# Two product steps moved behind each value product, and three transfers of the last head group issued at other places, in a gated attention and feed-forward kernel

## The chip, the cores and the metric

One Trainium2 chip, one of its cores. The number is the device time of one execution in microseconds. TensorE (PE) does the matrix products, VectorE (DVE), ScalarE (ACT) and GpSimd (POOL) the elementwise work, and SyncE (SP) only issues transfers. Each engine works through its own instructions strictly in the order in which the program issues them; an instruction that waits holds up everything behind it on that engine. POOL issues transfers too, so a transfer that must wait for its source stands in front of POOL's next elementwise work.

## What is computed

```python
def _A_ref(x, wqkv, wo):                     # S=2048, D=512
    H = 32; Dh = D // H; W = 256             # causal, window of 256
    scores = jnp.einsum("bhqd,bhkd->bhqk", q, k) * (Dh ** -0.5)
    mask = (idx[:, None] - idx[None, :] >= 0) & (idx[:, None] - idx[None, :] < W)
    p = _softmax(jnp.where(mask[None, None], scores, -1e9), axis=-1)
    return (heads of p @ v side by side) @ wo
def _B_ref(x, w_gate, w_up, w_down):         # F=1792
    return (_silu(x @ w_gate) * (x @ w_up)) @ w_down
g = _sigmoid((x * gate_w).sum(-1, keepdims=True))
return g * a + (1 - g) * b
```

All of it is in float32; the kernel splits operands into a high and a low half (`split`, line 67) and makes three products for one.

## The kernel before

Three stages follow each other. The **first** (to about 165 us) makes values, queries and keys. The **second** (to about 640 us) runs the attention of the 32 heads in 8 groups `g` of 4, and, between the attention's instructions, the products of x with `w_gate` and `w_up` for the feed-forward part. The **third** multiplies the hidden tiles with `w_down`, the attention with `wo`, and mixes both.

**The order of the second stage is written out by hand** (lines 793 to 826). `t` counts blocks of 128 positions over all groups, 16 a group; the last group, `g` = 7, is `t` = 112 to 127, and `t` = 128 only ends it. A block has four **ticks** (`hd` = 0 to 3); tick `k` is 4`t` + `hd`. In a tick the program issues, in this order: one score tile for finding the row maxima of the next group (`s1`, `stage1`, line 595, product into a bank `pc`, reduced by DVE in line 597); one score tile of this group (`s2`, `stage2`, line 634, into one of two banks `pd`, then ACT's exponential in line 636 into a tile `pt`, then POOL's masks on a pair of heads in lines 638 and 641); some **steps** of the feed-forward products (line 556); and at the end whatever was booked for this tick (`tick_end`). In the last group there is no `s1`, and `s2` comes two at a time in ticks 0 and 2.

**A step** is two products of 512 columns, one on each half of PE's 128 rows ("lanes"). The score tiles also take half of the rows each, `s1` and `s2` opposite halves. `DEAL` (lines 791, 792) says how many steps each tick gets; in the first block of four they are `1, 2, 0, 1` for groups 0 to 6, and two in every tick for the last group.

**The value product** (`av`, line 656) multiplies the masked `pt` tiles of up to six blocks with the values, for 512 positions at a time. It is issued in tick 1 of every fourth block, behind that tick's steps. It fills two banks: one of the `pc` kind and, before the last group, one of the two `pd` banks that `s2` uses. `evacuate` (line 661) follows: ACT copies the second bank to `ob` (line 667), the two are added to `oe` (for `g` = 7 by DVE, line 669), and POOL issues the store of `oe` to the tensor `od` (line 675). So 32 value products are made, 27 of them with a `pd` bank.

**Sums and inverses.** One row in 17 of what a value product makes is the softmax's sum. `invert` (line 454) reads the sums of 512 positions back from `od` (`den`, line 456), takes the reciprocal (line 458) and stores it to `rd` (line 459); both transfers are issued by POOL. In the last group `INV[c]` does this for chunks `c` = 0 and 1, booked at ticks 4(117 + 4`c`) + 3 and 12 ticks later (lines 766 to 768). The chunks 2 and 3 follow in the third stage.

**The odd sum.** `lanes` deals the feed-forward sums over two lanes of 64 rows. One sum is left over: its lane-1 half is made at the very start of the stage and put in the tensor `spill` (line 526); its lane-0 half comes at the very end (block 125 on). When its first product is issued, the program takes a `kept` buffer and has POOL load `spill` into it (lines 552, 553); `odd_end` adds the two (DVE, line 530).

**Also in POOL's queue in the last group:** the low halves of the last weights (`wl`, line 72), stores of the last unit's sums (line 501), and loads of `w_down` into buffers of the last weights (`wd_raw`, line 782), three of them booked for tick 502, in block 125. Two of those three go into the buffers (`wh`, `wl`) of the unit whose last step is the last step of the stage.

Of the kernel before, what the change touches and what calls it, by code (L numbers as in the profile page):

```python
# [9 lines left out]
F32 = mybir.dt.float32  # L10
# [6 lines left out]
P = 128  # L17
S, D, H, DH, W, F = 2048, 512, 32, 16, 256, 1792
NK = D // P
NB = S // P  # L20
CH = 512
NCH = S // CH
G = H // 4
# [10 lines left out]
def gated_mix(ctx, tc, xT, xn, wqk, wv, wo, wgu, wd, gw, out):  # L34
# [4 lines left out]
    nc = tc.nc  # L39
# [8 lines left out]
    od = dram.tile([G, P, S], F32, name="od")  # L48
    raws = dram.tile([NF, 2, NCH, P, CH], F32, name="raws")
    spill = dram.tile([P, CH], F32, name="spill")  # L50
# [36 lines left out]
    def run(gen, n=None):  # L87

        while n is None or n > 0:
            if next(gen, run) is run:  # L90
                break
            n = n and n - 1
# [19 lines left out]
    def bank(n):  # L112
        names = BANKS[n if isinstance(n, str) else ("pa", "pb", "pc", "pd")[n]]
        names.append(names.pop(0))
        return psum.tile([P, CH], F32, name=names[-1])
# [338 lines left out]
    def invert(c, pool):  # L454
        den = pool.tile([P, P], F32, name="den")
        nc.gpsimd.dma_start(den, shares[:, c * CH:(c + 1) * CH].rearrange("h (q i) -> h q i", q=4))
        yield
        nc.vector.reciprocal(den, den)
        nc.gpsimd.dma_start(rd[c].rearrange("h (q i) -> (h q) i", q=4), den)
        yield  # L460

# [6 lines left out]
    with ExitStack() as A:  # L468
        sm = A.enter_context(tc.tile_pool(name="sm", bufs=2))
        osb = A.enter_context(tc.tile_pool(name="osb", bufs=1))  # L470
        ptp = A.enter_context(tc.tile_pool(name="ptp", bufs=13, side="right"))

        def kept():
            return sm.tile([P, CH], F32, name="ev", bufs=EV)
# [5 lines left out]
        def later(n, *fs):  # L480
            AT.setdefault(NOW[0] + n, []).extend(fs)

        def at(k, *fs):
            AT.setdefault(k, []).extend(fs)
# [8 lines left out]
        def products(key, c):  # L493
            wh, wl = WT[key]
            return [(wt[:, k], xt[c][:, k]) for k in range(NK) for wt, xt in ((wh, xhi), (wh, xlo), (wl, xhi))]

        def copy_out(key, c, ps):
            place = kept()
            queue = nc.gpsimd if key == UNITS[-1] else nc.sync
            later(0, lambda: nc.scalar.copy(place, ps))  # L500
            later(3, lambda: queue.dma_start(raws[key[1], key[2], c], place))
# [10 lines left out]
        LAG, PART = 3 * NK + 6, []  # L512

        def lanes():


            turn, sums = 3 * NK, [(key, c) for key in UNITS[1:] for c in range(NCH)]
            odd = sums.pop(NCH - 1)
            ps, turned = {odd: bank("pa")}, {}
            rows = (sums + [odd], [odd] + [None] + sums)  # L520
            starts = [[turn * o for o in range(len(sums) + 1)], [0, turn] + [turn * o + LAG for o in range(len(sums))]]

            def odd_start(ps):
                place = kept()
                later(0, lambda: nc.scalar.copy(place, ps))
                later(3, lambda: nc.sync.dma_start(spill, place))

            def odd_end(ps):
                place, rest = kept(), PART.pop()
                later(0, lambda: nc.vector.tensor_tensor(out=place, in0=ps, in1=rest, op=ALU.add))  # L530
                later(3, lambda: nc.gpsimd.dma_start(raws[odd[0][1], odd[0][2], odd[1]], place))

            def items(lane):
                for at_, o in zip(starts[lane], rows[lane]):
                    while o and len(lines[lane]) < at_:
                        lines[lane].append(None)
                    if o:
                        lines[lane].extend((o, i) for i in range(turn))

            lines = [], []  # L540
            items(0)
            items(1)
            for both in zip_longest(*lines):
                for lane, item in enumerate(both):
                    if item is None:
                        continue
                    o, i = item
                    first = o is odd or not lane
                    if first and i == 0 and not (lane and o is odd):
                        ps[o] = bank("pa")  # L550
                        if o is odd:
                            PART.append(kept())
                            nc.gpsimd.dma_start(PART[0], spill)
                    w, x = products(*o)[i]
                    r = slice(64 * lane, 64 * lane + 64)
                    mm = nc.tensor.matmul(ps[o], w[r], x[r], start=first and i == 0,  # L556
                                          stop=(o is odd or bool(lane)) and i == turn - 1)
                    if not first and i == 0:
                        tc.add_manual_dep(mm.ins, BEHIND[turned.pop(o)].ins.name, SYNC, reason="the other rows are summed")
                    if i < turn - 1:  # L560
                        continue
                    if o is odd:
                        (odd_start if lane else odd_end)(ps.pop(o))
                    elif not lane:
                        turned[o] = len(BEHIND)
                    else:
                        copy_out(*o, ps.pop(o))
                        n = sums.index(o) + 1
                        if n == len(sums) or sums[n][0] != o[0]:
                            later(3, prepare)  # L570
                yield
# [89 lines left out]
        def evacuate(g, c):  # L661

            first, second = AV[g, c]
            lo = 0 if c else 64
            e = osb.tile([P, CH], F32, name="oe", bufs=2)
            o = osb.tile([P, CH], F32, name="ob")
            nc.scalar.copy(o[:, lo:], second[:, lo:])  # L667
            if g == G - 1:
                nc.vector.tensor_tensor(out=e[:, lo:], in0=first[:, lo:], in1=o[:, lo:], op=ALU.add)
                if lo:  # L670
                    nc.vector.tensor_copy(e[:, :lo], first[:, :lo])
            else:
                nc.vector.tensor_copy(e, first)
                nc.gpsimd.tensor_tensor(out=e[:, lo:], in0=e[:, lo:], in1=o[:, lo:], op=ALU.add)  # L674
            nc.gpsimd.dma_start(od[g, :, c * CH:(c + 1) * CH], e)

# [43 lines left out]
        def wd_early(k, f, piece):  # L722
            at(k, lambda: later(4, load_wd(f, pieces[piece], kept())))
# [33 lines left out]
        g7 = (G - 1) * NB  # L757
# [4 lines left out]
        for b in range(NB):  # L762
            at(4 * (17 + 4 * b) + 2, lambda b=b: gate_block(b))
        at(4 * (g7 + 2), gate_end)
        INV = [invert(c, osb) for c in range(2)]
        for c in range(2):
            for n in range(2):
                at(4 * (g7 + 5 + 4 * c) + 3 + 12 * n, lambda c=c: run(INV[c], 1))
        at(4 * g7, put_pieces)
        for m in range(8):  # L770
            wd_early(4 * (g7 + 1 + m) + 2, m, m)
        for n in range(2):
# [16 lines left out]
            spread(4 * (16 * g + 17) + 1, 1, stack(g + 2, 1))  # L789

        DEAL = [[[(hd + 1) * n // 4 - hd * n // 4 for hd in range(4)] for n in deal] for deal in ((4, 9, 9, 8), (8, 8, 8, 8))]
        DEAL[0][0] = 1, 2, 0, 1
        for t in range(G * NB + 1):
            g, i = divmod(t, NB)
            d, part = divmod(t, NSLOT)
            s1 = stage1(g + 1, i) if t < g7 else iter(())
            s2 = stage2(g, i) if t < G * NB else iter(())
            values = part == 0 and t > 0
            for hd in range(4):
                k = NOW[0] = NSLOT * t + hd  # L800
                if not (values and hd == 2):
                    run(s1, 1)
                if t < g7:
                    run(s2, 1)
                elif hd % 2 == 0:
                    run(s2, 2)
                if t == G * NB and hd == 0:
                    last_tile = tile_silu(2)
                    run(last_tile, 1)
                if t < G * NB:  # L810
                    run(steps, DEAL[t >= g7][part][hd])
                if hd == 1 and values:
                    run(s1, 1)
                    av(*divmod(d - 1, NCH))
                    while UNDER:
                        UNDER.pop(0)()
                    evacuate(*divmod(d - 1, NCH))
                tick_end()
            if i in (7, 15) and g + 1 < G:
                UNDER.append(lambda g=g, i=i: put_max(g + 1, i // 8))  # L820
            if t >= 10 and t % 4 == 2 and t + 6 < G * NB:
                load_v((t + 6) // 4)
# [196 lines left out]
```

## Time and profile before

| | us |
|---|---|
| median of 3 runs | 842.83 (842.41 to 843.29) |
| the profiled execution, as a run | 846.21 |
| its span, first to last instruction | 844.5 |
| PE busy | 824.5 |
| PEld (weight loads) busy | 692.8 |
| DVE, ACT, POOL busy | 552.2, 472.8, 402.5 |
| mean granted TensorE clock | 0.997 |

The profiled execution took 846.21 us, 1.71 more than its span and 3.38 more than the median run. Line numbers are those of the kernel before. In a row of the timeline stand start, duration, engine, line, operation, out<-in, shape, count and, in brackets, how long the engine was idle before it and what ended that. In a row of the waits stand who waited for whom, the total, how often, and the longest. A busy time of PE overlaps the next product's start, so PE's lost time is read from starts, not from the busy share.

### The profile page before, as it was taken

Reading aid. Unit: us, or ns where it says so; the run is one execution under the profiler, and the core shown is the slowest. Engines: PE = TensorE matmul, PEld = TensorE weight load, DVE = VectorE, ACT = ScalarE, POOL = GpSimd, SP = SyncE. Lnnn points to the kernel's source line nnn. Section 1 sums busy time; section 2 is a strip of 40 time slices with the busy share of each in tenths; the row PEclk is TensorE's granted clock in tenths of the full one; section 3 lists DMA queues with packets and bytes.
Section 4 is the critical chain, followed back from the end, with each engine's and each line's share of the span. In section 5 each row is a group of like instructions: output and inputs, shape, how many; then the busy total and the mean of one; then the engine's idle time right before and its main releaser. Section 6 shows DMA issues by size and latency. Waiting matters only on the chain.

```text
span 844.5 us, 20512 instructions
## 1 busy us (share of the span) xinstructions
PE 824.5 (98%) x7681; PEld 692.8 (82%) x7681; DVE 552.2 (65%) x1425; ACT 472.8 (56%) x956; POOL 402.5 (48%) x716
## 2 busy tenths in 40 slices
PE   9999999999999999999999999999987999999998
PEld 7888888888888888888888888888765888888886
DVE  5675554158786877878878778784473657564652
ACT  7454553222676776766767667676664563433431
POOL 5124441441465666766667666666664015352220
PEclk9999999999999999999999999999999999999999
DMA  8456676386534564545645455433638797878611
GB/s 295 142 174 224 231 263 217 132 274 198 169 117 153 194 205 149 191 147 199 205 158 185 154 165 180 148 122 114 209 117 297 279 283 218 258 228 256 204 59 50
DMA packets 80147, 159.70 MB, mean 189 GB/s; under 512 B 14960, under 2 KB 19440, under 8 KB 80048
## 3 DMA queue, kind: packets, MB, share of 16 engines
q1 hardware_dynamic: 68400, 127.18, 45.1%
q0 software_dynamic: 11072, 30.17, 11.0%
q8 instruction: 60, 0.98, 0.5%
q10 hardware_dynamic: 576, 1.05, 0.4%
q14 instruction: 39, 0.32, 0.1%
HBM read 93.32 MB, written 65.01 MB: 187 GB/s over the span
## 4 chain that ended last, share of the span: by engine, by line
PE 91%; POOL 2%; ACT 2%; issue 2%; DMA 1%; SPq 0%; DVE 0%; ACTq 0%; DVEq 0%; POOLq 0%
PE pa L556 20%; PE pb L556 10%; PE pd L634 6%; PE pc L656 4%; PE pd L381 4%; PE pb L381 4%; PE pa L381 4%; PE pd L83 3%; PE pc L595 3%; PE pc L83 3%; PE pc L82 3%; PE pc L81 3%; PE pd L82 3%; PE pd L81 3%; PE pb L656 2%
## 5 line engine op out<-in xcount | busy, mean ns | idle before, releaser
L636 ACT ACTIVATE pt<-pd 128x384 f32<-128x384 f32 (+2 forms) x512 | 233.0, 475 | 50.0 <-PE pc L595 12.5
L597 DVE CUSTOM_DVE_ANT_0 pc<-pc,mask 128x384 f32<-128x384 f32 (+2 forms) x322 | 172.4, 544 | 41.7 <-PE pc L595 22.2
L634 PE MATMUL pd<-q,k 64*128 64x384 f32 (+2 forms) x512 | 174.1, 352 | 9.5 <-ACT ob L667 6.8
L556 PE MATMUL pa<-xhi,wh 64*128 64x512 f32 x492 | 160.7, 398 | 0.0
L556 PE MATMUL pa<-xhi,wl 64*128 64x512 f32 x492 | 157.7, 393 | 0.0
L556 PE MATMUL pa<-xlo,wh 64*128 64x512 f32 x492 | 157.4, 393 | 0.0
L638 POOL TENSOR_SCALAR_AFFINE_SELECT pt<-pt 128x256 f32<-128x256 f32 x256 | 108.0, 422 | 75.9 <-ACT pt L636 74.1
L634 PEld LDWEIGHTS pd<-q,k 64*128 64x128 f32 x512 | 93.2, 184 | 35.2 <-ACT ob L667 14.8
L595 PE MATMUL pc<-k,q 63*128 63x384 f32 (+2 forms) x322 | 103.2, 327 | 0.0
L641 POOL TENSOR_SCALAR_AFFINE_SELECT pt<-pt 128x256 f32<-128x256 f32 x224 | 97.3, 434 | 0.0
L556 PE MATMUL pb<-xhi,wh 64*128 64x512 f32 x244 | 97.1, 398 | 0.0
L597 DVE CUSTOM_DVE_ANT_0 pb<-pb,mask 128x384 f32<-128x384 f32 (+2 forms) x158 | 86.2, 546 | 15.3 <-PE pb L595 10.0
L556 PE MATMUL pb<-xlo,wh 64*128 64x512 f32 x244 | 96.0, 394 | 0.0
L556 PE MATMUL pb<-xhi,wl 64*128 64x512 f32 x244 | 95.8, 392 | 0.0
L556 PEld LDWEIGHTS pa<-xhi,wh 64*128 64x128 f32 x492 | 80.2, 185 | 2.1 <-DVE mx L597 0.5
L556 PEld LDWEIGHTS pa<-xhi,wl 64*128 64x128 f32 x492 | 79.6, 185 | 1.7
L556 PEld LDWEIGHTS pa<-xlo,wh 64*128 64x128 f32 x492 | 79.5, 186 | 1.2
L904 DVE TENSOR_TENSOR sg<-got,sg 128x512 f32<-128x512 f32 x53 | 45.4, 857 | 46.2 <-ACT sg L903 38.7
L597 DVE DVE_READ_ACCUMULATOR2_ANT mx<- 128x1 f32 x512 | 72.5, 142 | 0.0
L656 PE MATMUL pd<-pt,vg 64*32 64x320 f32 (+4 forms) x1184 | 63.1, 346 | 0.0
L674 POOL TENSOR_TENSOR oe<-oe,ob 128x512 f32<-128x512 f32 (+1 forms) x28 | 35.1, 1254 | 55.9 <-ACT ob L667 52.4
L595 PEld LDWEIGHTS pc<-k,q 63*128 63x128 f32 x322 | 58.7, 184 | 3.6 <-DVE mx L597 0.4
(306 smaller groups left out, 2046.3 us busy)
## 6 DMA issues: line engine op xcount, KB each, us to landing
got<-raws SPq DMA_DIRECT2D x106, 256.0 KB
raws<-ev SPq DMA_DIRECT2D x91, 256.0 KB
q<-xd SPq DMA_DIRECT2D x96, 128.0 KB
k<-xd SPq DMA_DIRECT2D x96, 128.0 KB
xd<-cx SPq DMA_DIRECT2D x16, 512.0 KB
xd<-cy SPq DMA_DIRECT2D x16, 512.0 KB
od<-oe POOLq DMA_DIRECT2D x32, 256.0 KB, 3.1
raw<-wgu SPq DMA_DIRECT2D x25, 256.0 KB
```

The source lines that it names most:

```text
L81: nc.tensor.matmul(ps, lh, rh, start=start and i == 0, stop=False, skip_group_check=skip)
L82: nc.tensor.matmul(ps, lh, rl, start=False, stop=False, skip_group_check=skip)
L83: nc.tensor.matmul(ps, ll, rh, start=False, stop=stop and i == n - 1, skip_group_check=skip)
L381: nc.tensor.matmul(ps, l[:, w], r[:, k], start=n in (1, 2, 5) and k == m == 0, stop=k == 1 and m == 2, skip_group_check=True)
L556: mm = nc.tensor.matmul(ps[o], w[r], x[r], start=first and i == 0, stop=(o is odd or bool(lane)) and i == turn - 1)
L595: nc.tensor.matmul(ps[:, :n], QT[g % 2][pr][r, q0:q0 + P], KT[g % 2][pr][r, k0:k0 + n], start=True, stop=True)
L597: mx = nc.vector.tensor_tensor_reduce(out=ps[:, :n], in0=ps[:, :n], in1=mask[:, 3 * P - n:], scale=1.0, scalar=NEG, op0=ALU.add, op1=ALU.m ...
L634: nc.tensor.matmul(ps[:, :n], KT[g % 2][pr][r, k0:k0 + P], QT[g % 2][pr][r, k0:k0 + n], start=True, stop=True)
L636: BEHIND.append(nc.scalar.activation(pt[:, j, :n], ps[:, :n], AF.Exp, scale=SCALE))
L638: nc.gpsimd.affine_select(out=pt[:, :, :P], in_=pt[:, :, :P], pattern=[[0, 2], [1, P]], compare_op=ALU.is_ge, fill=0.0, base=0, channel_mu ...
L641: nc.gpsimd.affine_select(out=pt[:, :, 2 * P:], in_=pt[:, :, 2 * P:], pattern=[[0, 2], [-1, P]], compare_op=ALU.is_ge, fill=0.0, base=-1, ...
L656: nc.tensor.matmul(AV[g, c][h][32 * j:32 * j + 32, q0 - c * CH:q1 - c * CH], VG[4 * g + kb // 4][o, kb % 4, 17 * j:17 * j + 32], PT[g, kb, ...
```

## The change

Three edits and one that goes with them.

1. `DEAL[0][0]` becomes `1, 1, 2, 0`: of the four steps around a value product of groups 0 to 6, one goes from ahead of it (tick 1) and one from tick 3 to tick 2, behind that tick's score tile. In the last group nothing of this changes.
2. The odd sum's first half is read back at tick 4(112 + 8) = 480 by SP, into a buffer `xn` that is otherwise used for x rows, in place of POOL's load at block 125 into a `kept` buffer.
3. The store of `oe` is booked instead of issued at once: in the last group 4 ticks after the value product's tick, in the others for the end of the same tick.
4. `invert` yields between the reciprocal and the store, and the last group books it at 0, 12 and 15 ticks in place of 0 and 12: load, reciprocal, and the store three ticks later.

```diff
         nc.vector.reciprocal(den, den)
+        yield
         nc.gpsimd.dma_start(rd[c].rearrange("h (q i) -> (h q) i", q=4), den)
...
                         ps[o] = bank("pa")
-                        if o is odd:
-                            PART.append(kept())
-                            nc.gpsimd.dma_start(PART[0], spill)
...
-            nc.gpsimd.dma_start(od[g, :, c * CH:(c + 1) * CH], e)
+            later(4 if g == G - 1 else 0, lambda: nc.gpsimd.dma_start(od[g, :, c * CH:(c + 1) * CH], e))
...
         for c in range(2):
-            for n in range(2):
-                at(4 * (g7 + 5 + 4 * c) + 3 + 12 * n, lambda c=c: run(INV[c], 1))
+            for n in (0, 12, 15):
+                at(4 * (g7 + 5 + 4 * c) + 3 + n, lambda c=c: run(INV[c], 1))
         at(4 * g7, put_pieces)
+        def put_back():
+            PART.append(osb.tile([P, D], F32, name="xn", bufs=2))
+            nc.sync.dma_start(PART[0], spill)
+
+        at(4 * (g7 + 8), put_back)
...
-        DEAL[0][0] = 1, 2, 0, 1
+        DEAL[0][0] = 1, 1, 2, 0
```

## The prediction, made before the changed kernel had run

> **What bounds the kernel now.** I read the page's chain of work first, then the waits, then the timeline of single value products and of the last group.
>
> ```profile
> span 844.5 us, 20512 instructions
> PE 91%; POOL 2%; ACT 2%; issue 2%; DMA 1%; SPq 0%; DVE 0%; ACTq 0%; DVEq 0%; POOLq 0%
> ```
> ```profile
> PE pd L634 <- ACT ob L667: 6.8, 27, 0.5
> ...
> DVE ev L530 <- DMA ev<-spill: 4.9, 1, 4.9
> ...
> PE pd L634 <- ACT pt L636: 2.6, 2, 2.2
> ```
>
> PE sets the end nearly everywhere, and POOL for some 2%. One wait recurs 27 times, once for each value product that takes a `pd` bank: the score tile behind it waits for ACT's copy `ob`. The third value product, typical of half of them, on PE and then on ACT:
>
> ```profile
> 253.97 0.39 PE L556 MATMUL pb<-xhi,wl 64*128 64x512 f32 x1
> ...
> 254.47 0.45 PE L656 MATMUL pc<-pt,vg 64*32 64x320 f32 x1
> ...
> 256.75 0.27 PE L656 MATMUL pd<-pt,vg 64*32 64x128 f32 x1
> 256.95 0.44 PE L634 MATMUL pd<-q,k 64*128 64x384 f32 x1
> 257.23 0.34 PE L595 MATMUL pc<-k,q 63*128 63x384 f32 x1
> 257.78 0.44 PE L634 MATMUL pd<-q,k 64*128 64x384 f32 x1 [0.21 <-ACT ob L667]
> 257.79 0.49 PE L556 MATMUL pa<-xhi,wh 64*128 64x512 f32 x1
> 258.06 0.39 PE L556 MATMUL pb<-xhi,wh 64*128 64x512 f32 x1
> 258.17 0.44 PE L634 MATMUL pd<-q,k 64*128 64x384 f32 x1
> ...
> 258.47 0.39 PE L556 MATMUL pb<-xlo,wh 64*128 64x512 f32 x1
> ```
> ```profile
> 253.84 0.50 ACT L636 ACTIVATE pt<-pd 128x384 f32<-128x384 f32 x1
> ...
> 257.14 0.59 ACT L667 COPY ob<-pd 128x512 f32<-128x512 f32 x1 [2.42 <-PE pd L656]
> 257.62 0.50 ACT L636 ACTIVATE pt<-pd 128x384 f32<-128x384 f32 x1
> ```
>
> Behind the product (last start 256.75) there are two gates, not one. `s2` of tick 3 starts at 257.78, when the copy has ended (257.14 + 0.59 = 257.73); `s2` of the next block's tick 0 starts at 258.17, when the exponential behind that copy has ended (257.62 + 0.50 = 258.12). Between 256.95 and 258.47 PE gets one step done where the spacing of steps would allow far more:
>
> ```profile
> 585.14 0.44 PE L634 MATMUL pd<-q,k 64*128 64x384 f32 x2
> 585.42 0.39 PE L556 MATMUL pa<-xlo,wh 64*128 64x512 f32 x1
> ...
> 585.65 0.39 PE L556 MATMUL pa<-xhi,wl 64*128 64x512 f32 x1
> ```
>
> That is the last group, where steps do follow the score tiles behind the product: one each 0.23 us.
>
> **The steps around the value product.** Two steps in tick 2 take 2 x 0.23 = 0.46 us from about 257.23 on (by the last group's rows, 0.28 behind `s2`), so `s1` of tick 3 moves to about 257.69. The gate at 257.78 has not moved, so these two steps lie wholly under the copy. Tick 3 now has no step, and the next `s2` still waits for 258.17. So at 258.47 PE stands at the same place of the program as before: the one step that used to lie between the gates, and the one from ahead of the product, now both lie in the hole. What is gained is only what the value product **starts** earlier, since one step less (0.23 us) stands ahead of it, and the copy, the exponentials and both gates move with it.
>
> How much it can start earlier is set by the bank that it takes: the `pd` bank of tick 0's `s2`, free when its exponential has ended. Here that is 253.84 + 0.50 = 254.34; with the 0.05 us between the copy's end and 257.78, the product can start at 254.39 or 254.40 in place of 254.47: a gain of 0.07, not 0.23. ACT has a copy of a feed-forward sum just ahead of this exponential in every second value product, so 14 of the 27 are like this. The fourth is the other kind:
>
> ```profile
> 266.55 0.49 ACT L636 ACTIVATE pt<-pd 128x384 f32<-128x384 f32 x1 [0.33 <-PE pd L634]
> ```
> ```profile
> 267.34 0.45 PE L656 MATMUL pb<-pt,vg 64*32 64x320 f32 x1
> ```
>
> Its bank is free at 267.04, 0.30 us before the product, so the whole 0.23 is gained. Read in the same way, nine are like this, three can gain about 0.12 (a weight cast is ahead of the exponential), one nothing. Sum: 14 x 0.07 + 9 x 0.23 + 3 x 0.12 = 3.4 us. Bounds: 27 x 0.03 = 0.8 if the gate takes nearly all, 27 x 0.23 = 6.2 if ACT's order leaves the exponentials earlier. I take 3.4, since the ends of the exponentials are measured.
>
> **POOL in the last group.** First the store of `oe` with its wait, then the load of the sums, the masks behind it and the product that reads them; then the chain's end.
>
> ```profile
> 599.20 0.56 POOL L675 DMA_DIRECT2D od<-oe  x1 [3.02 <-DVE oe L671]
> ...
> 603.21 0.56 POOL L456 DMA_DIRECT2D den<-od  x1
> 603.78 0.42 POOL L638 TENSOR_SCALAR_AFFINE_SELECT pt<-pt 128x256 f32<-128x256 f32 x1
> ...
> 607.67 0.58 POOL L641 TENSOR_SCALAR_AFFINE_SELECT pt<-pt 128x256 f32<-128x256 f32 x1
> ...
> 631.55 0.56 POOL L459 DMA_DIRECT2D rd<-den  x1 [4.69 <-ACT pt L636]
> ...
> 634.46 0.56 POOL L553 DMA_DIRECT2D ev<-spill  x1
> ...
> 635.55 0.54 POOL L782 DMA_DIRECT2D wh<-wd  x1
> ...
> 637.91 1.23 POOL L638 TENSOR_SCALAR_AFFINE_SELECT pt<-pt 128x256 f32<-128x256 f32 x2
> ```
> ```profile
> 607.96 0.45 PE L656 MATMUL pc<-pt,vg 64*32 64x320 f32 x1
> ...
> 634.06 0.39 PE L556 MATMUL pa<-xhi,wl 64*128 64x512 f32 x1
> ...
> 637.10 0.40 PE L656 MATMUL pc<-pt,vg 64*32 64x256 f32 x1 [1.40 <-POOL pt L638]
> ...
> 639.20 0.24 PE L656 MATMUL pb<-pt,vg 64*32 64x64 f32 x1 [0.50 <-POOL pt L638]
> ...
> 650.05 0.50 PE L81 MATMUL pd<-q,hh 128*128 128x512 f32 x1 [1.94 <-ACT hh L69]
> ```
>
> The stage ends on POOL: the store of the inverses holds the queue for 4.69 us until the reciprocal is there, and masks, a store, the `spill` load (0.56) and the `w_down` loads follow back to back, so the last value product waits at 637.10 and 639.20. The change takes the store (0.56), its wait and the `spill` load from ahead of the masks. But the waits do not go by 4.69 + 1.1: the `wh` load goes into the buffer of the last weights, so it cannot be issued before the last step's end, 634.06 + 0.39 = 634.45, and the last masks stand behind it. It goes from 635.55 to about 634.5, and the end of the value product moves by the same **1.05 us**. Below, this could be 0 (if another queue entry holds POOL as long); above, the 1.90 of both waits. I take 1.05.
>
> The reading of `spill` by SP costs one issue on a queue with room; DVE's wait of 4.9 us for it goes too, but nothing that PE needs before 639 stands behind it. The booked stores of groups 0 to 6 stay in POOL's order but for things booked for the same tick, and nobody reads them before the third stage: zero; if POOL had no room there, 28 x 0.56 would only be moved, not added.
>
> One edit **adds** a wait. The store of `oe` is now two ticks ahead of the load of the sums instead of six, and that load waits for the store to land:
>
> ```profile
> DMA to landing us min/median/max: 2.4/3.1/4.5
> ```
>
> One pair of masks (0.42 each) lies between, so the store would be issued at about 603.21 - 0.8 - 0.5 = 601.9 and lands at 605.0 (604.3 to 606.4): `den` is held for 1.8 us (1.1 to 3.2). Behind it on POOL the masks run without a break from 603.78 to 608.25, so the last pair ends near 610.05. The value product of 607.96 lasts 2.3 us (as 254.47 to 256.75) and reads that pair in its last third, from about 609.6. PE loses 0.45; bounds 0 and 1.9. The second chunk has the same order, but POOL recovers before its next product: 0 to 1. I take 0.5 in all.
>
> [...]
>
> **The start of the third stage** has a hole of 1.94 us before 650.05, since the second hidden tile's load lands late in a crowded stretch. A 256 KB store of a sum and a `w_down` load leave this stretch for earlier, so the hole may shrink: 0 to 1.9, I take 0.5.
>
> Sum: -3.4 - 1.05 + 0.5 - 0.5 = **-4.4 us**: 844.5 to 840.1 of span, 842.83 to **838.4** for the runs. The profiled execution is 1.7 longer than its span; I take the difference over to the median as it stands.
>
> **Rivals.**
>
> *The wait is only exchanged.* The value product does not start earlier (its bank, or POOL's mask of its last block, holds it) and the last group's gain is eaten by `den`: -0.8 - 1.05 + 1.9 = about 0: 842.8. For it: 14 of 27 show the bank free only 0.13 before the start. Against: nine are free 0.30 before.
>
> *More than forecast.* All 27 products gain 0.23 (6.2) and the hole of 1.94 goes: 6.2 + 1.05 + 1.9 - 0.5 = 8.7: 834.2. After that hole PE's granted clock drops:
>
> ```profile
> 652.00:654.00 2.00, 2.00 (x6) 1.61 (x5) 1.73 (x3) 1.84 (x4) 0.00 (x0) 0.50 1.05 419
> ```
>
> Six products in 2 us at a clock of 0.50, where 0.23 each would give 8.7: 2.7 x 0.23 = 0.6 us more to win in this stretch, 833.6, if the hole becomes too short for it. [...]
>
> *Slower: POOL behind `den`.* At chunks 0 and 1 the load of the sums holds POOL for up to 3.2 us each, and both delays reach PE in full, 6.4; with the steps at their lower bound and 1.05 that is +4.5: 847.4. It decides once the store lands later than about 4 us and POOL finds no idle time before the next product. Against: the waits of 3.02 us for `oe`, which stood in POOL's queue, go.
>
> **How the numbers follow.** Forecast (836.5 to 840.5) 0.50; more than forecast (below 836.5) 0.22; exchanged 0.18, of which 0.04 still ends below 841.1; slower 0.10. Two runs of this kernel can be told apart by about 0.2%, 1.7 us. So faster 0.76, same 0.14, slower 0.10. The range is 834.2, the rival above, to 842.6, just short of no gain.
>
> **What would show it.** The 27 waits of L634 for `ob` all but vanish, and those of L634 for the exponential rise from 2 to some 29, about 0.3 us each. Two steps stand between `s2` and `s1` behind each product; the products' distances shrink by 0.07 and 0.23 in turn. POOL's 4.69 goes, `wh<-wd` is issued at the last step's end, `den<-od` shows a wait of about 1.8. It is wrong if the distances do not shrink, or shrink by 0.23 throughout, or if POOL's wait at `den` reaches PE.

## The result, and the profile after

| | before | after |
|---|---|---|
| median of the runs (17 and 17) | 842.98 (841.41 to 845.68) | 839.33 (836.17 to 842.92) |
| ratio, 95% interval | | 0.9955 (0.9943 to 0.9968) |
| the profiled execution, as a run | 846.21 | 840.21 |
| its span | 844.5 | 838.5 |
| mean granted TensorE clock of it | 0.997 | 0.992 |

The change saves 3.65 us, where 4.4 were forecast. The two profiled executions lie 6.0 apart, more than the medians, since the one of before is 3.2 above its median and the one of after 0.9. Lines of the changed kernel: steps L554, `s2` L632, exponential L634, masks L636 and L639, value product L654, `ob` L665, `oe` L667, its store L673 (two lower than before each); the store of the inverses L460, the `w_down` loads L785.

The page of the changed kernel: its span, the clock in 40 slices of 21 us, and the chain of work.

```profile
span 838.5 us, 20514 instructions
...
PEclk9999999999999999999999999999997999999999
...
PE 97%; DVE 1%; ACT 1%; DMA 1%; POOL 0%; issue 0%; DVEq 0%; ACTq 0%; POOLq 0%
```

POOL's 2% of the chain are gone, PE has 97%. One slice, the 31st (629 to 650 us), has a clock of 0.7, which no slice of before's page had. A row each of the waits of the changed kernel, first PE's, then POOL's:

```profile
PE pd L632 <- ACT pt L634: 2.7, 2, 2.3
```
```profile
POOL den L456 <- DMA od<-oe: 4.2, 1, 4.2
```

The 27 waits for `ob` (6.8 us) have no row any more, and neither has DVE's wait for `spill`. The waits for the exponential stay at two. New is POOL's wait of 4.2 for the store of `oe`.

The third value product again, on PE and on ACT:

```profile
253.75 0.44 PE L654 MATMUL pc<-pt,vg 64*32 64x320 f32 x1
253.89 0.45 PE L654 MATMUL pd<-pt,vg 64*32 64x320 f32 x1
...
256.15 0.27 PE L654 MATMUL pd<-pt,vg 64*32 64x128 f32 x1
256.35 0.44 PE L632 MATMUL pd<-q,k 64*128 64x384 f32 x1
256.36 0.50 PE L554 MATMUL pb<-xhi,wl 64*128 64x512 f32 x1
...
257.18 0.44 PE L632 MATMUL pd<-q,k 64*128 64x384 f32 x1
...
257.57 0.44 PE L632 MATMUL pd<-q,k 64*128 64x384 f32 x1
257.64 0.43 PE L554 MATMUL pb<-xlo,wh 64*128 64x512 f32 x1
```
```profile
253.34 0.88 ACT L634 ACTIVATE pt<-pd 128x384 f32<-128x384 f32 x2
256.54 0.59 ACT L665 COPY ob<-pd 128x512 f32<-128x512 f32 x1 [2.33 <-PE pd L654]
257.02 1.13 ACT L634 ACTIVATE pt<-pd 128x384 f32<-128x384 f32 x2
```

Both gates still stand, at the same distance from the copy `ob`: 256.54 + 0.59 = 257.13, and `s2` starts at 257.18; the exponential ends at about 257.02 + 0.50 = 257.52, and the next `s2` starts at 257.57. They have no bracket now, because steps and the other score tiles run up to them. The `pd` half of the product starts at 253.89, 0.05 behind the end of the exponential (253.34 + about 0.50); its other half needs no such bank and starts 0.14 sooner.

The last group, POOL:

```profile
597.63 0.56 POOL L673 DMA_DIRECT2D od<-oe  x1
...
603.19 0.56 POOL L456 DMA_DIRECT2D den<-od  x1 [4.22 <-DMA od<-oe]
```
```profile
628.08 0.56 POOL L460 DMA_DIRECT2D rd<-den  x1 [2.44 <-DVE den L458]
...
630.34 0.54 POOL L785 DMA_DIRECT2D wh<-wd  x1 [1.16 <-PE pb L554]
...
631.42 0.77 POOL L636 TENSOR_SCALAR_AFFINE_SELECT pt<-pt 128x256 f32<-128x256 f32 x2
```

and PE there, from the product that `den` delays to the end of the stage:

```profile
603.57 2.43 PE L654 MATMUL pc<-pt,vg 64*32 64x320 f32 x74
606.37 0.53 PE L654 MATMUL pc<-pt,vg 64*32 64x64 f32 x22 [0.37 <-POOL pt L636]
...
625.19 0.39 PE L554 MATMUL pb<-xlo,wh 64*128 64x512 f32 x1
627.91 0.85 PE L632 MATMUL pd<-q,k 64*128 64x256 f32 x2 [2.34 <-ACT pt L634]
...
632.63 0.62 PE L554 MATMUL pa<-xhi,wl 64*128 64x512 f32 x1
633.18 0.74 PE L654 MATMUL pc<-pt,vg 64*32 64x320 f32 x1
```

From 627.91 on everything on PE is slow: a step's product takes 0.62 in place of 0.39, one of the value product 0.74 in place of 0.45. The windows say why (columns: busy time and count of PE, weight loads, DVE, ACT and POOL, then the clock, the share of the DMA engines, GB/s); the first fence is the changed kernel, the second the kernel before.

```profile
626.00:628.00 2.00, 0.09 (x1) 0.09 (x1) 1.97 (x4) 1.04 (x3) 0.00 (x0) 0.98 0.16 66
628.00:638.00 10.00, 10.00 (x117) 6.76 (x118) 2.31 (x4) 4.76 (x12) 5.26 (x11) 0.50 0.48 166
638.00:640.00 2.00, 2.00 (x9) 1.68 (x9) 1.29 (x2) 0.92 (x2) 0.58 (x2) 0.96 0.51 155
```
```profile
628.00:638.00 10.00, 6.39 (x91) 4.25 (x95) 5.03 (x7) 5.60 (x13) 6.41 (x14) 1.00 0.30 104
```

The clock is 0.50 through 628 to 638 and a little beyond both ends: (1 - 0.98) x 2 / 0.5 = 0.08 ahead and (1 - 0.96) x 2 / 0.5 = 0.16 behind, 10.24 us in all. It begins as PE comes out of 2.34 us of idleness, in which ACT's `s2` exponentials are late. Before had the same hole (a PE start at 628.79, the next 2.60 later) and kept a clock of 1.00:

```profile
631.38 0.66 PE L634 MATMUL pd<-q,k 64*128 64x256 f32 x2 [2.21 <-ACT pt L636]
```

What holds ACT is DVE, in the changed kernel:

```profile
621.99 3.35 DVE L740 RECIPROCAL ev<-ev 128x512 f32<-128x512 f32 x1
...
626.23 0.69 DVE L742 TENSOR_TENSOR ev<-q,ev 128x512 f32<-128x512 f32 x1
```
```profile
626.96 0.62 ACT L69 CAST q<-ev 128x512 fp32r<-128x512 f32 x1 [2.74 <-DVE ev L742]
```

ACT's part of splitting the second early hidden tile (`tile_early`, booked at tick 4(112 + 10) + 15) stands in its queue ahead of the exponentials and waits 2.74 us for the chain behind a reciprocal of 3.35. In the kernel before it waits 2.62 us there (the cast starts at 630.43).

Where the 6.0 us between the two profiled executions went is read from the first and last row of single value products:

| | before | after | difference |
|---|---|---|---|
| start of the 28th product | 582.66 | 578.26 | -4.40 |
| 28th to 31st start | 38.61 | 39.41 | +0.80 |
| 31st to 32nd start | 13.11 | 15.51 | +2.40 |
| 32nd product, first to last start | 5.07 | 4.18 | -0.89 |
| from there to the end | 205.05 | 201.14 | -3.91 |

### The profile page after: what moved, and what is told of

Its sections match the earlier page's. It is cut to its first block, busy times and chain, and to the rows that moved or that the text cites. A ratio compares the mean times of both kernels' runs of the same rounds, so it can differ in the third digit from the quotient of the medians.

```text
span 838.5 us, 20514 instructions
## 1 busy us (share of the span) xinstructions
PE 829.0 (99%) x7681; PEld 703.8 (84%) x7681; DVE 554.9 (66%) x1425; ACT 471.7 (56%) x956; POOL 400.3 (48%) x715
## 3 DMA queue, kind: packets, MB, share of 16 engines
q10 hardware_dynamic: 576, 1.05, 0.4%
## 4 chain that ended last, share of the span: by engine, by line
PE 97%; DVE 1%; ACT 1%; DMA 1%; POOL 0%; issue 0%; DVEq 0%; ACTq 0%; POOLq 0%
PE pa L554 21%; PE pb L554 10%; PE pd L632 7%; PE pc L654 4%; PE pd L381 4%; PE pb L381 4%; PE pa L381 4%; PE pc L593 3%; PE pd L654 3%; PE pd L81 3%; PE pc L83 3%; PE pc L82 3%; PE pd L82 3%; PE pd L83 3%; PE pc L81 3%; PE pb L654 2%
## 5 line engine op out<-in xcount | busy, mean ns | idle before, releaser
L634 ACT ACTIVATE pt<-pd 128x384 f32<-128x384 f32 (+2 forms) x512 | 232.3, 474 | 52.5 <-PE pd L632 12.2
L632 PE MATMUL pd<-q,k 64*128 64x384 f32 (+2 forms) x512 | 177.1, 358 | 2.9 <-ACT pt L634 2.7
L554 PE MATMUL pa<-xhi,wl 64*128 64x512 f32 x492 | 161.7, 399 | 0.0
L554 PE MATMUL pa<-xlo,wh 64*128 64x512 f32 x492 | 160.1, 397 | 0.0
L554 PE MATMUL pa<-xhi,wh 64*128 64x512 f32 x492 | 159.0, 396 | 0.0
L636 POOL TENSOR_SCALAR_AFFINE_SELECT pt<-pt 128x256 f32<-128x256 f32 x256 | 108.1, 423 | 77.6 <-ACT pt L634 75.6
L632 PEld LDWEIGHTS pd<-q,k 64*128 64x128 f32 x512 | 93.9, 185 | 25.8 <-ACT pt L634 9.9
L554 PE MATMUL pb<-xhi,wl 64*128 64x512 f32 x244 | 97.2, 398 | 0.0
L554 PE MATMUL pb<-xlo,wh 64*128 64x512 f32 x244 | 96.7, 396 | 0.0
L554 PE MATMUL pb<-xhi,wh 64*128 64x512 f32 x244 | 96.3, 395 | 0.0
L639 POOL TENSOR_SCALAR_AFFINE_SELECT pt<-pt 128x256 f32<-128x256 f32 x224 | 95.7, 427 | 0.0
L554 PEld LDWEIGHTS pa<-xhi,wl 64*128 64x128 f32 x492 | 81.1, 186 | 1.5
L554 PEld LDWEIGHTS pa<-xhi,wh 64*128 64x128 f32 x492 | 80.1, 186 | 2.5 <-DVE mx L595 0.5
L554 PEld LDWEIGHTS pa<-xlo,wh 64*128 64x128 f32 x492 | 80.0, 186 | 1.4
L907 DVE TENSOR_TENSOR sg<-got,sg 128x512 f32<-128x512 f32 x53 | 41.8, 788 | 45.6 <-ACT sg L906 39.8
L654 PE MATMUL pd<-pt,vg 64*32 64x320 f32 (+4 forms) x1184 | 62.9, 345 | 0.0
```

Source lines behind the costliest of these rows:

```text
L632: nc.tensor.matmul(ps[:, :n], KT[g % 2][pr][r, k0:k0 + P], QT[g % 2][pr][r, k0:k0 + n], start=True, stop=True)
L634: BEHIND.append(nc.scalar.activation(pt[:, j, :n], ps[:, :n], AF.Exp, scale=SCALE))
L636: nc.gpsimd.affine_select(out=pt[:, :, :P], in_=pt[:, :, :P], pattern=[[0, 2], [1, P]], compare_op=ALU.is_ge, fill=0.0, base=0, channel_mu ...
L639: nc.gpsimd.affine_select(out=pt[:, :, 2 * P:], in_=pt[:, :, 2 * P:], pattern=[[0, 2], [-1, P]], compare_op=ALU.is_ge, fill=0.0, base=-1, ...
L654: nc.tensor.matmul(AV[g, c][h][32 * j:32 * j + 32, q0 - c * CH:q1 - c * CH], VG[4 * g + kb // 4][o, kb % 4, 17 * j:17 * j + 32], PT[g, kb, ...
```

## The experiments

The medians are of this kernel and of before on the same chip. "28th" is the start of the 28th value product in the profiled execution, ahead of the transfers' edits in the last group (the stores of groups 0 to 6, booked for the end of their tick, come before it: e2 has them and starts at 582.36, before at 582.66); executions with the same order of steps differ there by up to 0.5 (577.92 to 578.41 in seven of them). The length of a product is taken from its first start to its last.

| | median (runs) | before (runs) | ratio, 95% interval | 28th | 30th product, length | last product, start and length | span |
|---|---|---|---|---|---|---|---|
| e1 steps alone | 838.32 (6) | 843.66 (29) | 0.9938 (0.9921 to 0.9955) | 578.00 | 2.28 | 632.04, 4.18 | 836.7 |
| e2 the rest alone | 843.47 (12) | 843.66 (29) | 1.0002 (0.9987 to 1.0018) | 582.36 | 3.20 | 636.20, 4.18 | 841.5 |
| e3 one in each tick | 840.69 (12) | 843.66 (29) | 0.9958 (0.9943 to 0.9974) | 578.80 | 3.32 | 634.02, 4.18 | 839.4 |
| e4 two ahead still | 842.42 (12) | 843.66 (29) | 0.9990 (0.9978 to 1.0003) | 581.69 | 3.08 | 635.97, 2.28 | 839.3 |
| e5 sums read later | 838.60 (6) | 843.37 (17) | 0.9948 (0.9930 to 0.9965) | 578.24 | 2.29 | 630.09, 2.29 | 835.1 |
| e6 split later | 837.81 (6) | 843.37 (17) | 0.9932 (0.9918 to 0.9946) | 578.41 | 3.34 | 628.55, 4.57 | 837.6 |
| e7 both of these | 835.95 (6) | 843.37 (17) | 0.9920 (0.9905 to 0.9936) | 577.93 | 2.28 | 626.96, 4.57 | 834.3 |
| e8 before, split later | 842.32 (11) | 843.37 (17) | 0.9991 (0.9982 to 0.9999) | 582.46 | 2.29 | 631.48, 7.59 | 841.6 |
| e9 e7, loads later | 837.54 (6) | 843.01 (16) | 0.9940 (0.9922 to 0.9958) | 578.14 | 2.28 | 627.25, 4.34 | 835.8 |
| e10 steps, split later | 839.35 (11) | 843.01 (16) | 0.9959 (0.9947 to 0.9972) | 577.92 | 2.28 | 627.03, 7.62 | 840.3 |

**The steps alone, and the rest alone.** e1 is the kernel before with this edit, e2 the changed kernel with it undone:

```diff
-        DEAL[0][0] = 1, 2, 0, 1
+        DEAL[0][0] = 1, 1, 2, 0
```

> The kernel before with the new deal of steps alone (1, 1, 2, 0). Theory: the steps bring the gain of groups 0 to 6, so the 28th value product, the first of block 112, starts at about 578.3 us of the trace (582.66 before, 578.26 in the changed kernel); the last group and the start of the third stage stay as before, with POOL's wait of 4.7 us at the store of the inverses and the hole of about 2 us at the third stage's start, so the time is about 4.4 us below before. Rival: the gain is made in the last group, and the time is within 1 us of before.

> The changed kernel with the old deal of steps (1, 2, 0, 1): the transfers' edits alone. Theory: the 28th value product starts at 582.7 as before; POOL waits about 4 us at the load of the sums and the 30th value product lasts about 0.8 us longer; the last product ends about 1 us earlier and the hole at the third stage's start goes, but PE's clock may be halved behind the wait of about 2.3 us in block 126; in all between 3 us faster and 1 us slower than before. Rival: the transfers carry the gain, and it is 4 us faster.

The steps carry all of it: 0.9938 alone, against 0.9955 for the whole change, and the rest alone is 1.0002. PE's waits in e2 have the row of before again:

```profile
PE pd L632 <- ACT ob L665: 6.7, 27, 0.5
PE pd L632 <- ACT pt L634: 2.7, 2, 2.4
```

Yet in e2 the transfers did what they were to do: POOL's wait of 4.69 is gone, the masks behind the `w_down` loads begin at 634.87 and 636.16 (before: 636.62 and 637.91), and the last product no longer waits for POOL. In e2's profiled execution that gain went into the 30th product (3.20 in place of 2.28) and into a clock that is halved for a while behind the hole in block 126:

```profile
628.00:638.00 10.00, 7.64 (x67) 5.04 (x71) 5.78 (x7) 5.16 (x14) 7.14 (x16) 0.79 0.48 166
638.00:650.00 12.00, 12.00 (x121) 9.11 (x102) 5.18 (x8) 6.36 (x12) 3.75 (x7) 0.89 0.77 273
```

**Earlier start, or a filled hole?** Two other deals of the same four steps in the changed kernel: e3 takes one step from ahead of the product but leaves one in tick 3; e4 leaves two ahead and moves tick 3's.

```diff
-        DEAL[0][0] = 1, 1, 2, 0
+        DEAL[0][0] = 1, 1, 1, 1
```

> The changed kernel with the deal 1, 1, 1, 1: still one step less ahead of the value product, but only one in tick 2 and one between the two gates. Theory (the gain is the product's earlier start): the 28th value product starts at 578.3 within 0.5 us, as in the changed kernel, and the time is the same within 1 us. Rival (the gain is the second step in the hole behind the product): the start is at about 580.5 and the time 2 us above the changed kernel.

```diff
-        DEAL[0][0] = 1, 1, 2, 0
+        DEAL[0][0] = 1, 2, 1, 0
```

> The changed kernel with the deal 1, 2, 1, 0: the two steps ahead of the product stay, the step of tick 3 goes to tick 2. Theory (the gain is the product's earlier start): nothing is gained, the 28th value product starts at about 582.5, and the time is about 4 us above the changed kernel. Rival (a step in the hole behind the product is what counts): half is gained, 580.5, and about 2 us above the changed kernel.

PE's waits in e4, whose 28th product starts only 0.67 us sooner than in e2:

```profile
PE pd L632 <- ACT pt L634: 2.7, 2, 2.4
...
PE pd L632 <- ACT ob L665: 0.3, 1, 0.3
```

Of the 27 waits one is left, and next to nothing is gained: a step put into the wait takes it from the table without moving the gate. What gains is the step taken from ahead of the product: e3's 28th product starts at 578.80, 3.56 before e2's. Moving tick 3's step as well adds 578.80 - 578.26 = 0.54 (0.67 by e4), barely more than two executions with one order of steps differ.

**The load of the sums.** The prediction let `den` wait for a store just issued. e5 books that load six ticks later:

```diff
-            for n in (0, 12, 15):
+            for n in (6, 12, 15):
```

> The changed kernel with the load of the sums booked 6 ticks later (6, 12, 15 in place of 0, 12, 15), so that the store of the sums has landed when POOL comes to it. Theory: POOL's wait of 4.2 us at that load goes, the 30th value product lasts 2.3 us again in place of 3.1, and the time is about 0.8 us below the changed kernel. Rival (POOL finds room before the product is held up by something else): no gain.

```profile
597.60 0.56 POOL L673 DMA_DIRECT2D od<-oe  x1
...
603.52 0.56 POOL L456 DMA_DIRECT2D den<-od  x1 [1.03 <-ACT pt L634]
604.10 0.42 POOL L636 TENSOR_SCALAR_AFFINE_SELECT pt<-pt 128x256 f32<-128x256 f32 x1
```

In e5 the load is issued at 603.52, hardly later than the changed kernel's 603.19, but POOL does not stand still until then: masks have gone ahead of it. The 30th product is back at 2.29, so the 0.8 us were this wait. The profiled execution of e5 kept its clock:

```profile
625.00:635.00 10.00, 7.93 (x127) 6.11 (x128) 5.73 (x9) 6.72 (x15) 5.86 (x13) 1.00 0.56 186
```

It has the hole (7.93 of 10 us busy) without the halved clock, so the two executions price the clock in the changed kernel: 15.51 against 13.26 us from the 31st to the 32nd product and 4.18 against 2.29 in the last, 4.1 us. (In e1 and e3, with a clock of 0.52 over 626 to 636 and of 0.53 over 628 to 638, the same two stretches take 15.38 and 15.51, and 4.18 each.) Of these 1.6 come back, as the third stage takes 202.72 in e5 and 201.14 there: with 0.8, the 3.4 us between the two spans. The clock was not switched by this edit, though: e5's six runs have mean clocks from 0.993 (span 840.3) to 1.000 (835.1), the 17 of the changed kernel from 0.992 to 1.000 (the two at 1.000 have spans of 834.5 and 835.3, the four at 0.995 or less 838.5 to 841.2).

**The hole in block 126.** e6 books ACT's and DVE's last part of the second early hidden tile six ticks later, where only two exponentials are still behind it on ACT; e7 adds e5's edit; e8 is the kernel before with e6's.

```diff
-        for n, ticks in enumerate(((1, 3, 3, 3, 3, 12), (7, 9, 9, 9, 9, 15))):
+        for n, ticks in enumerate(((1, 3, 3, 3, 3, 12), (7, 9, 9, 9, 9, 21))):
```

> The changed kernel with the split of the second early hidden tile booked 6 ticks later (21 in place of 15), so that ACT does not wait for DVE's reciprocal in block 125. Theory: the hole of about 2.3 us on PE in block 126 goes, and with it the halved clock of 6.8 to 10.2 us that begins at its end; 3 to 5 us below the changed kernel, 834 to 836, runs closer together, mean clock 0.998 or more. Rival (the clock falls for the waits of the value product or by chance): the halved clock stays and the gain is 2.3 us at most.

> Both: the load of the sums 6 ticks later and the split 6 ticks later. Theory: the two gains add up, 4 to 6 us below the changed kernel, 833 to 835.5. Rival: POOL's queue was hidden behind the hole, and nothing is added to the split alone.

> The kernel before with the split booked 6 ticks later and nothing else. Theory: here the end of the last group is set by POOL, which waits 4.7 us for the reciprocal at the store of the inverses; the hole of 2.2 us in block 126 goes but the last value product still waits for POOL's masks, so the gain is under 1.5 us. Rival (the hole is on the path in the kernel before too): 2 to 5 us faster.

The windows of e7:

```profile
625.00:635.00 10.00, 8.62 (x125) 5.66 (x122) 5.57 (x9) 5.20 (x11) 6.85 (x14) 1.00 0.59 182
635.00:645.00 10.00, 8.51 (x38) 6.67 (x37) 5.50 (x9) 5.98 (x11) 2.20 (x5) 1.00 1.04 396
```

Hole and halved clock are both gone from this stretch in e6 and e7, and the mean clocks of e7's six runs are 0.998 or 1.000. (In e6's profiled execution the clock is 0.57 over 644 to 648, at the start of the third stage, where PE waits 0.8 us for `hh` and 0.7 for `hl`.) e7 is the best of all: 835.95, 7.4 us under before and with an interval below the whole change's. In e8 the same edit is worth only 1 us (0.9991): there the last product starts at 631.48, but lasts 7.59, waiting for POOL:

```profile
PE pc L656 <- POOL pt L638: 1.8, 1, 1.8
...
PE pc L656 <- POOL pt L641: 1.0, 2, 0.5
```

**What the transfers' edits are worth without the hole.** e10 is e1 with the later split; against e6 and e7 it lacks only the transfers' edits (and e7's later load).

> The kernel before with the steps of the change and the split of the second early hidden tile six ticks later; none of the transfers' edits. Theory (the transfers' edits were worth nothing only because ACT's hole in block 126 covered POOL's delay; without the hole POOL sets the end again): the hole before block 126's score tile is gone, but the last value product waits for POOL's masks and lasts 6 to 8 us; it ends near 635 in place of 631.5 with the transfers' edits; median 838 to 839.5, ratio about 0.994 to 0.995, no faster than the steps alone (838.3). Rival (the transfers' edits are worth nothing in any company): median 835 to 836.5, ratio about 0.991.

POOL in e10, then in e7, both with the last product starting near 627.0:

```profile
626.89 0.56 POOL L459 DMA_DIRECT2D rd<-den  x1 [4.69 <-ACT pt L636]
...
631.62 0.78 POOL L638 TENSOR_SCALAR_AFFINE_SELECT pt<-pt 128x256 f32<-128x256 f32 x2
```
```profile
626.94 0.56 POOL L460 DMA_DIRECT2D rd<-den  x1 [2.44 <-DVE den L458]
...
629.11 0.77 POOL L636 TENSOR_SCALAR_AFFINE_SELECT pt<-pt 128x256 f32<-128x256 f32 x2
```

The masks come 2.5 us sooner with the edits and the product ends at 626.96 + 4.57 = 631.53 in place of 627.03 + 7.62 = 634.65. The clock, 0.81 over 625 to 635 in e10 and 1.00 in e7, has little part in this: POOL's last masks end at 634.15 in e10 and at 631.22 in e7, 2.9 us apart. So the edits are worth 3.1 us at the end of this stage (which of them does how much was not separated), and by the ratios 0.9959 against 0.9932 (e6) and 0.9920 (e7); beside the hole they are worth nothing (e2). The later split by itself gains nothing without them (e10 is no faster than e1). That lower clock makes the span of e10's profiled execution overstate this.

**The loads behind the last masks.** e9 is e7 with two loads of `w_down` two blocks later, as in e7 the last product still waits 1.3 us at a mask.

```diff
-((13, "raw"), (13, "wh"), (13, "wl"), (17, "wh"), (17, "wl"))
+((13, "raw"), (15, "wh"), (15, "wl"), (17, "wh"), (17, "wl"))
```

> The load of the sums six ticks later and the split of the second early hidden tile six ticks later, as in the run that had both, and in addition the `wh` and `wl` loads of w_down booked two blocks later (block 127 in place of 125), so that POOL's last masks no longer stand behind a `wh` load that waits for the odd sum. Theory (the last value product's wait of 1.75 us for a mask is the queue behind that load): the product starts about as before, near 627, but lasts under 3.5 us in place of 4.57, its end comes 1 to 1.75 us earlier; the median is 834.2 to 835.3, ratio about 0.990 to 0.991. Rival (the start of the third stage is bound by transfers, so what arrives earlier waits there): the hole ahead of the first w_down products grows from 1.9 to 3 us or more and the median stays at 835.5 to 837.

A miss: the first masks are free at 628.34 (e7: 629.11), but the product now waits twice, 1.01 and 0.83 us between starts, and lasts 4.34, so the wait has mostly changed its place. Both waits end with a mask: the two last pairs of masks take 1.10 and 1.30 us in place of e7's 0.77 and 0.82, and end at 631.27, where e7's end at 631.22. Why they take longer stays open. The third stage pays:

```profile
639.86 0.39 PE L83 MATMUL pc<-q,k 128*128 128x512 f32 x1
642.95 0.50 PE L81 MATMUL pd<-q,hh 128*128 128x512 f32 x1 [2.71 <-ACT hh L69]
```

The hole there is 3.1 us from start to start (e7: 640.26 to 642.15, 1.9), and 837.54 is no better than e7. ACT, for which PE waits here, itself waits 4.09 us for a load of feed-forward sums (`got<-raws`), with the DMA engines at a share of 1.02 in this stretch (e7: 1.04): what e9 wins ahead of it waits for this load.

## Why the prediction was right, point by point

The forecast of 838.4 was met to 0.9 us, but partly by luck, because misses cancelled. Of the 4.4 us forecast, 3.4 were the steps' and 1.05 came from the transfers and the third stage. By e1 the steps alone bring some 5 us, by e2 the rest brings nothing that is clear of noise.

- **The product's earlier start: right, in mechanism and size.** Forecast 3.4, with the exponential's end as the gate; e3 against e2 measures 3.56. The `pd` half starts 0.05 behind that end, as forecast. From copy `ob` to copy the distances shrink by 0.17 to 0.26 in the nine products of the fourth's kind (forecast 0.23), and by 0.08 to 0.15 in those of the third's but the first (forecast 0.07); the next point is in these too.
- **"At 258.47 PE stands at the same place of the program as before": this step failed, by little.** Between before and after the two gates move by 0.60 at the third product, and the step `pb<-xlo,wh` behind them by 258.47 - 257.64 = 0.83. The step moved out of tick 3 no longer holds its lane when the second gate opens. So this move, put at nothing, is worth some 0.5 to 0.7 us over 27 products by e3 and e4 (hardly more than the 0.5 by which executions differ), and the whole term is 4.4 in place of 3.4 (582.66 - 578.26).
- **That the waits for the exponential would rise to 29: wrong.** They stay at 2. The gate is there, but PE has other work up to it, and a wait is only booked where the engine is idle.
- **`den`: right in kind, mis-sized.** Forecast a hold of 1.8 us and 0.45 on PE; measured 4.22 and 0.80. The store took 5.0 us from the end of its issue (598.19) to the release of the load (603.19), where the median landing of 3.1 stood in the sum. The DMA engines were at a share of 0.88 to 1.06 from 598 to 604 us; that this is why the store took so long was not tested. That only 0.80 of 4.22 reached PE is POOL's slack. At the second chunk POOL stands idle for 2.6 us ahead of the load (before: 0.3), and the 31st product is as long as before, 2.28: the prediction's "0 to 1" is 0.
- **"The `wh` load cannot be issued before the last step's end": this step failed.** It waits for `pb`, the odd sum's lane-0 half, which ends near 630.4; the last step starts at 632.63. So the buffer is not, as was said of POOL's queue ahead of the prediction, that of the unit whose step ends the stage. The masks come forward by more than 1.05: by 2.5 us in e7 against e10, and the product's end by 3.1. In the changed kernel this did not show, because block 126's hole and the clock behind it came first.
- **The start of the third stage: forecast 0.5, and 3.9 in the profiled executions.** Not because of the transfers moved out of it: e1, without the transfers' edits, needs 200.49 us from its last product to the end, the changed kernel 201.14. PE came to it late, at half clock, and so the load was there. In e5 and e7, with the clock whole, the hole is back (2.04 and 1.89 between starts), and 202.72 and 202.73 us are no less than the 202.51 of e8, which lacks the transfers' edits. So no run shows the 0.5.
- **What no term had: the halved clock in block 126.** The prediction considered it only behind the third stage's hole, and passed over the hole in block 126, which stands in its own table of waits (L634 for the exponential, longest 2.2). The clock costs some 4.1 us where it lasts 10.24, less 1.6 that come back, and it took what the first, second and fifth point gave more than forecast: -4.4 + 0.8 + 2.4 - 0.9 - 3.9 = -6.0 against the profiled execution of before. The two runs with a clock of 1.000 took 836.2 and 837.0, on either side of 836.5, the border of the rival "more than forecast".
- The rival of the exchanged wait falls with e3, that of POOL behind `den` with the 0.80 and with e5.

## What to carry to other kernels

A wait that recurs is not a loss of that size: e4 took 26 of its 27 entries away for a ratio of 0.9990 (0.9978 to 1.0003); look for what moves the gate behind it, here the start of the product whose copy the gate waits for. Before a stall on one engine is worked on, look for an idle hole of another cause in the same place: the transfers' edits were worth nothing beside the hole in block 126 and 3 us without it, and the later split was worth about 1 us without them. A load that reads back what the same queue has just stored belongs some ticks later, behind work that needs no such wait: here the load waited 4.22 us on POOL and PE lost 0.80, which e5 got back.

## What the runs showed of the hardware that was not expected

In the changed kernel the granted clock was 0.50 for 10.24 us behind a hole of 2.34 us of idle PE, on work that then ran without a break (10.00 of 10 us busy); e2's two windows give (0.21 x 10 + 0.11 x 12) / 0.5 = 6.8, and e4's profiled execution, with the same hole, about 3.4:

```profile
628.00:638.00 10.00, 7.64 (x110) 5.92 (x109) 5.03 (x7) 4.96 (x12) 6.38 (x14) 0.83 0.47 168
```

(0.17 x 10 / 0.5). Before and e5 kept 1.00 with the same hole. The table has the profiled executions with this hole. The time at half clock is worked out from the windows named, in the same way; for e1 and e3 it is the part that lies in the one window.

| | PE's wait in the hole | granted clock in the windows | time at half clock |
|---|---|---|---|
| e4 | 2.4 | 0.83 over 628 to 638, 1.00 over 638 to 650 | 3.4 |
| e2 | 2.4 | 0.79 over 628 to 638, 0.89 over 638 to 650 | 6.8 |
| changed kernel | 2.34 | 0.98 over 626 to 628, 0.50 over 628 to 638, 0.96 over 638 to 640 | 10.24 |
| e3 | 2.3 | 0.53 over 628 to 638 | 9.4 |
| e1 | 2.2 | 0.52 over 626 to 636 | 9.6 |
| e5 | 2.3 | 1.00 over 625 to 635 | none |
| before | 2.21 | 1.00 over 628 to 638 | none |

The hole is 2.2 to 2.4 us in all seven, and its length does not order them: the two with 2.4 have the shortest halvings, and 2.21 and 2.3 stand beside a whole clock as well as beside a halved one (e1, e3). The third stage shows no order either: before's clock was 0.50 over 652 to 654, behind a wait of 1.94, while e9's was 1.00 over 635 to 645, with a wait of 2.71 in it. What decides whether the clock falls, and for how long, was not shown, and no run could set it.
